# A stream of weight jobs spread over the attention tiles, with another last tile for its planner

## The chip, the cores and the metric

The kernel runs on one core of a Trainium2 chip. The metric is the device time of one execution in microseconds (us), lower is better. One execution was recorded by the hardware profiler; its times are counted from the first instruction of the span.

## The reference

Attention with rotary embedding (4 batches, 8 heads, 576 positions, head size 64), then a layer that takes the maximum of three products, then a layer with SiLU. All weights are dense; no routing takes place.

```python
q_rot, k_rot = rotate(q), rotate(k)
scores = scale * np.matmul(q_rot, k_rot.transpose(0, 1, 3, 2))
attn = np.exp(scores - max(scores)) ; attn = attn / (sum(attn) + 1e-09)
x = matmul(attn, v)                       # as 2304 tokens x 512
h = np.maximum(np.maximum(x @ w1, x @ w2), x @ w3)     # 512 -> 768
y = h @ w_out                                          # 768 -> 512
g = y @ w_in ; g = g * (1.0 / (1.0 + np.exp(-g)))      # 512 -> 2048
out = g @ w_out2                                       # 2048 -> 512
```

## The kernel before

Products that need accuracy are done as three passes of 16-bit floats: each operand is split into a high and a low part, and high x high, high x low and low x high are summed. Weights arrive as 64-bit floats, and are narrowed on the chip.

**The attention** is a list of 80 tiles, 20 for each batch: for a pair of heads and 128 queries a tile has scores on TensorE (`tile_scores`, L443, L433 and L434, in one PSUM tile s with a single buffer), the maximum on VectorE (`tile_max`, L453), exponentials on ScalarE (L460), the norm (`tile_norm`, L470 and L472), moves of the probabilities by SP's DMA queue (`tile_move`, L511), a transpose within blocks on VectorE (`tile_flip`, L533) and the product with the values (`av`, tile xp, L578). `attention()` is a generator; at step j it issues the scores and the maximum of tile j and the later parts of the tiles before it. It has five steps more than tiles, for the parts that trail. From tile 25 on (`LOOSE`) the scores of a tile are queued behind the last matmul group that was issued before.

**The first layer** of earlier batches runs between the tiles: the main loop draws groups of matmuls (L673) from `moe_groups()`, from tile 25 on in portions of three passes, as far as a debt of TensorE columns (`pace`) allows. Rotations of later queries and keys (`rope_steps`, L366 to L370) run on GpSimd. The groups of the last batch run behind the loop, for the most part in PSUM tiles mg, which take the place of the attention's; the second layer (`moe2`) comes last.

**The weight jobs** are the stream that the change touches. `side_jobs()` yields them one by one, with their planned cost in ns of VectorE time:

- `narrow_w2(WI, ...)`: 32 units that bring the weight w_in of the second layer to 32 bits. A unit is a load (L874), a cast on ScalarE (L229), three operations on VectorE (L241, planned 420; L248 and L249, planned 820), a sum of squares on ScalarE (L155) and a store to DRAM (L845, or L850 for the second weight). At the end the scale of the weight is found: a row maximum wm on VectorE (L263), a transpose (L122), a maximum (L124) and a broadcast (L130) on TensorE, four small operations on VectorE, planned 600.
- `narrow_w2(WO, ...)`: the same for w_out, whose loads and stores are in GpSimd's queue, and between its units the 16 items of `prep_w8`: a load of za, sums on GpSimd (L989), two high parts on ScalarE (L966), two low parts on VectorE (L970, planned 730 each) and two stores of w8o (L997) to w8scr, where the second layer will read them.

**The planner** gives every step an allowance. `busy(j)` estimates VectorE's other work in step j, and `SIDE` is one constant for all steps: the whole planned cost of the jobs and of the other work, divided by the number of steps. In each step from `LOOSE` on the debt `side_debt` grows by `SIDE - fixed[j - 1]`, and jobs are issued as long as it is positive. What is left after the loop is issued at once:

```python
            if j > LOOSE:
                side_debt += SIDE - fixed[j - 1]
...
            drawn = j > LOOSE and side_debt > 0 and side_next is not None
            if drawn:
                side_debt -= max(side_next, 0)
...
    for _ in side:
        pass
```

The order in which an engine takes its instructions is settled before the run, by a scheduler that places what was issued along a timeline of its own; an engine then works through its queue in that order.

Of the kernel before, what the change touches and what calls it, by code (L numbers as in the profile page):

```python
# [22 lines left out]
def fused_kernel(  # L23
# [568 lines left out]
    tiles, events, first, x_ready, av_at = [], {}, {}, {}, {}  # L592
# [10 lines left out]
    for i, (b, hp) in enumerate(pairs):  # L603
        u = first[b, hp]
        if b > 1:
            j = first[b, 0] + 3 * hp - 7
# [18 lines left out]
    LOOSE = 25  # L625
    LAST = [(B - 1, hp, t) for hp in range(NP) for t in PARTS[1][2]]

    def attention():

        back = lambda j, n: tiles[j - n] if n <= j < len(tiles) + n else None  # L630
        for j in range(len(tiles) + 5):
            b_now[0] = int(j > LOOSE)
            if j < len(tiles):
                with tc.issue_after(last["group"]) if j > LOOSE else nullcontext():
                    tile_scores(tiles[j])
                tile_max(tiles[j])
            for n in (3, 2):
                key = back(j, n)
                if key and moved(key[0]) and n == 3 - (key in LAST):
                    tile_flip(key)  # L640
            for a in av_at.pop(j, ()):
                av(*a)
            key = back(j, 1)
            if key:
                tile_norm(key)
                if moved(key[0]):
                    tile_move(key)
            key = back(j, 2)
            if key:
                (tile_last if moved(key[0]) else tile_turn)(key)  # L650
            for f, a in events.pop(j, ()):
                f(*a)
            yield
# [696 lines left out]
    def side_jobs():  # L1350


        yield from narrow_w2(WI, wi2, "wi")
        items, n, done = prep_w8(1.7), 0, 0
        for cost in narrow_w2(WO, wo2, "wo"):
            yield cost
            n += cost < 0
            while done < n / 1.25:
                x = next(items, None)
                if x is None:  # L1360
                    break
                if x < 0:
                    done += 1
                else:
                    yield x
        yield from items

    def busy(j):


        half = lambda i: 0 <= i < len(tiles) and tiles[i][2] == 4
        full = lambda i: 0 <= i < len(tiles) and tiles[i][2] != 4
        ns = 1350 * full(j) + 750 * half(j) + 150 * (j <= len(tiles)) + 230 * half(j - 2) + 500 * len(av_at.get(j, ()))
        for n in (2, 3):
            if j - n < len(tiles) and n == 3 - (tiles[j - n] in LAST):
                ns += 700 if half(j - n) else 1240
        ns += sum({qk_turn: 700, v_max: 800, v_scale: 150, v_scale_b: 600}.get(x[0], 0) for x in events.get(j, ()))
        return ns + max(pace[j], 0) * 530 // 3840

    side, side_debt, side_next = side_jobs(), 0, -1  # L1380
    fixed = {j: busy(j) for j in range(LOOSE, len(tiles) + 5)}
    SIDE = (60 * 1240 + 32 * 730 + sum(fixed.values())) // len(fixed)
    for j, _ in enumerate(attention(), 1):
        step[0] = j
        if moe is None:
# [10 lines left out]
        if x_p.get(1) is not None:  # L1396
# [4 lines left out]
            if j > LOOSE:  # L1401
                side_debt += SIDE - fixed[j - 1]
        debt = min(debt + (pace[j - 1] if j > LOOSE else RATE), 3 * RATE)
# [104 lines left out]
```

## Time and profile before

| | |
|---|---|
| median of 3 runs | 981.9 us (979.5 to 985.38) |
| profiled execution | 979.38 us, span 977.7 us |
| TensorE busy | 899.6 us, 92% |
| VectorE busy | 714.6 us, 73% |
| ScalarE busy | 609.2 us, 62% |
| GpSimd busy | 469.1 us, 48% |
| mean granted TensorE clock | 0.980 |

A share of busy time is an average over stages. Engines are named PE (TensorE matmuls), PEld (TensorE weight loads), DVE (VectorE), ACT (ScalarE), POOL (GpSimd) and SP (SyncE, which issues DMAs). A tile's name without its number stands for all its buffers. Matmuls overlap, so that the duration of one is longer than the distance to the next.

### The profile page before, as it was taken

How to read it: one execution, taken by the hardware profiler on the slowest of the kernel's cores; microseconds unless marked ns; L12 is line 12 of the kernel's file. 1: busy time of each engine (PE TensorE's matmuls, PEld its weight loads, DVE VectorE, ACT ScalarE, POOL GpSimd, SP SyncE). 2: the span in 40 equal slices, each digit the busy share in tenths (PEclk: the TensorE clock that was granted, in tenths of full speed). 3: DMA queues.
4: the chain of work that ended last, by engine and by line, in shares of the span. 5: the costliest groups of instructions: out<-in, count | busy, mean ns of one | idle time of the engine just before them, and what ended most of it. 6: DMA issues, size and time to landing. Idle time of an engine off the chain costs nothing.

```text
span 977.7 us, 19067 instructions
## 1 busy us (share of the span) xinstructions
PE 899.6 (92%) x6802; PEld 667.8 (68%) x6802; DVE 714.6 (73%) x1271; ACT 609.2 (62%) x1405; POOL 469.1 (48%) x546
## 2 busy tenths in 40 slices
PE   3877998989999999999998498999998999999997
PEld 1443664656667566666655386788887888888886
DVE  6779887887788778877777856365786867856554
ACT  1988577757778678788777544363554545545342
POOL 6744584960335414322233635164486467464363
PEclk9798999999999999999999799999999999999999
DMA  6943034958878998889878862173543434424101
GB/s 152 286 142 107 17 109 125 192 120 174 189 174 185 223 173 193 215 162 190 204 194 210 294 214 88 42 227 126 163 156 99 134 121 135 122 90 135 61 1 44
DMA packets 173679, 146.30 MB, mean 150 GB/s; under 512 B 50960, under 2 KB 156176, under 8 KB 173584
## 3 DMA queue, kind: packets, MB, share of 16 engines
q1 hardware_dynamic: 167984, 131.77, 53.5%
q0 software_dynamic: 4096, 12.59, 4.5%
q8 instruction: 54, 0.88, 0.4%
q10 hardware_dynamic: 1504, 0.72, 0.3%
q14 instruction: 41, 0.34, 0.1%
HBM read 90.51 MB, written 26.21 MB: 119 GB/s over the span
## 4 chain that ended last, share of the span: by engine, by line
PE 50%; DMA 8%; DVE 8%; ACT 5%; SPq 3%; issue 3%; POOL 2%; DVEq 0%; ACTq 0%; POOLq 0%
PE m L1121 8%; PE m L673 8%; PE mb L1121 6%; PE c L1184 4%; PE a L1184 4%; PE b L1184 4%; DMA pt<-e 3%; PE mg L673 3%; PE s L443 2%; PE xp L578 2%; SPq L511 2%; PE d L1184 2%; ACT e L460 2%; DVE nb L453 2%; POOL gsum L1068 1%
## 5 line engine op out<-in xcount | busy, mean ns | idle before, releaser
L673 PEld LDWEIGHTS <-w 128*128 128x128 f16 x1632 | 159.6, 99 | 61.6 <-issue 17.5
L673 PE MATMUL m<-x,w 128*128 128x256 f16 (+1 forms) x1348 | 185.4, 287 | 8.8 <-DVE t L704 4.3
L1184 PEld LDWEIGHTS <-g 128*128 128x128 f16 x1485 | 146.0, 98 | 17.6
L1121 PEld LDWEIGHTS <-w8s 128*128 128x128 f16 x1344 | 131.1, 98 | 16.1 <-issue 0.9
L460 ACT ACTIVATE e<-s,nb 128x576 f32<-128x576 f32 x144 | 105.2, 735 | 38.6 <-DVE nb L453 35.1
L453 DVE TENSOR_REDUCE nb<-s 128x2 f32<-128x1152 f32 (+1 forms) x80 | 98.5, 1232 | 37.9 <-PE s L443 33.4
L472 ACT ACTIVATE e<-e,rec 128x576 f32<-128x576 f32 x144 | 104.0, 766 | 13.4 <-DVE rec L470 11.8
L366 POOL TENSOR_TENSOR w<-qk,sin_sb 128x512 f32<-128x512 f32 (+2 forms) x40 | 41.9, 1049 | 81.2 <-DMA qk<-in_q_dram 57.9
L443 PE MATMUL s<-T 64*128 64x512 f32 x256 | 77.6, 685 | 0.0
L578 PE MATMUL xp<-pt,vd 128*64 128x256 f32 (+1 forms) x512 | 76.1, 414 | 0.9 <-DVE pt L533 0.7
L533 DVE STREAM_TRANSPOSE pt<-pt 128x1024 f32<-128x1024 f32 (+1 forms) x60 | 67.5, 1127 | 7.4 <-DMA pt<-e 7.4
L1135 POOL TENSOR_TENSOR z<-t 128x256 f32<-128x256 f32 x32 | 27.2, 850 | 89.8 <-DVE t L1127 54.1
L874 POOL DMA_DIRECT2D z<-in_moe_w_out_dram x32 | 17.8, 555 | 107.0 <-ACT junk L155 24.4
L1073 DVE SCALAR_TENSOR_TENSOR g<-gsum,sg,g 128x1024 f16<-128x1024 f32 x36 | 49.1, 1371 | 22.5 <-ACT g L1072 22.1
L673 PE MATMUL m<-h,wo 128*128 128x256 f16 (+1 forms) x448 | 63.7, 290 | 0.4 <-POOL wo L175 0.3
L1072 ACT ACTIVATE g<-gsum,sg 128x1024 f16<-128x1024 f32 x36 | 40.8, 1141 | 37.1 <-POOL gsum L1068 37.1
L673 PEld LDWEIGHTS <-wo 128*128 128x128 f16 x512 | 50.1, 99 | 17.2 <-issue 2.7
L578 PEld LDWEIGHTS xp<-pt,vd 128*64 128x64 f32 x512 | 35.2, 136 | 32.8 <-issue 9.8
L1184 PE MATMUL c<-w,g 128*128 128x256 f16 x376 | 48.6, 276 | 0.0
L1184 PE MATMUL b<-w,g 128*128 128x256 f16 x376 | 48.5, 273 | 0.0
L1184 PE MATMUL a<-w,g 128*128 128x256 f16 x376 | 48.4, 274 | 0.0
L367 POOL TENSOR_TENSOR qk<-qk,cos_sb 128x512 f32<-128x512 f32 (+2 forms) x44 | 46.8, 1067 | 2.7
(268 smaller groups left out, 2009.6 us busy)
## 6 DMA issues: line engine op xcount, KB each, us to landing
w8s<-w8scr SPq DMA_DIRECT2D x64, 448.0 KB, 4.2
pt<-e SPq DMA_DIRECT2D x192, 128.0 KB, 4.1
z<-in_moe_w_in_dram SPq DMA_DIRECT2D x32, 256.0 KB, 3.7
z<-in_moe_w_out_dram POOLq DMA_DIRECT2D x32, 256.0 KB, 4.3
w8scr<-w8o SPq DMA_DIRECT2D x32, 256.0 KB, 3.8
w<-in_moe_w_dram SPq DMA_DIRECT2D x6, 768.0 KB, 5.4
wo<-in_moe_w_dram SPq DMA_DIRECT2D x6, 768.0 KB, 4.5
qk<-in_q_dram SPq DMA_DIRECT2D x32, 128.0 KB, 3.6
```

The lines of the kernel that those rows point to most:

```text
L366: tt(out=w4, in0=t4, in1=sin2, op=ALU.mult)
L367: tt(out=t4, in0=t4, in1=cos2, op=ALU.mult)
L443: last["s"] = last["score"] = nc.tensor.matmul(s[:, o:o + 512], qs[r], kt[r], start=True, stop=True).ins
L453: x = nc.vector.tensor_reduce(out=nb[:, 0:m], in_=both(s, 0, 960, 576) if m > 1 else s[:, 0:576], op=ALU.max, axis=AX.X, negate=True)
L460: x = nc.scalar.activation(out=e[:, HK[g]], in_=s[:, SK[g]], func=AF.Exp, bias=nb[:, g:g + 1], accum_out=sm[:, g:g + 1])
L472: nc.scalar.activation(out=e[:, HK[g]], in_=e[:, HK[g]], func=AF.Copy, scale=r[:, g:g + 1])
L533: nc.vector.transpose(out=x, in_=x)
L578: nc.tensor.matmul(xp[r, 0:n], v4[:, g, c, :], turned(c, g), start=False, stop=(c == 3))
L673: x = nc.tensor.matmul(ps[:, 0:n], l, r, start=(first and i == 0), stop=(not more and i == len(passes) - 1))
L1073: nc.vector.scalar_tensor_tensor(out=l, in0=x, scalar=sg_t[jb], in1=h, op0=ALU.mult, op1=ALU.subtract)
L1121: nc.tensor.matmul(o, l, r, start=(i == 0), stop=(i == len(passes) - 1))
L1184: x = nc.tensor.matmul(ps, l, r, start=first, stop=last_, skip_group_check=True)
```

## The change

The estimate of the other work is taken over the 80 tiles alone, and the five steps behind them count as free of other work (0). The whole cost now counts 61 units instead of 60 and both scales, and is divided by the 55 tiles from `LOOSE` on, instead of by the 60 steps from `LOOSE` on. The jobs, their order among themselves and the loop that draws them stay as they are.

```diff
     side, side_debt, side_next = side_jobs(), 0, -1
-    fixed = {j: busy(j) for j in range(LOOSE, len(tiles) + 5)}
-    SIDE = (60 * 1240 + 32 * 730 + sum(fixed.values())) // len(fixed)
+    fixed = [busy(j) for j in range(len(tiles))] + 5 * [0]
+    SIDE = (61 * 1240 + 32 * 730 + 2 * 600 + sum(fixed[LOOSE:])) // (len(tiles) - LOOSE)
     for j, _ in enumerate(attention(), 1):
```

## Rows read from the trace of the kernel before

**Rows 1.** Stretches: from:to and length, busy us, TensorE clock, DMA share, GB/s.

```profile
205.00:524.00 319.00, 313.49 (x2110) 201.25 (x2110) 253.41 (x484) 247.94 (x697) 99.24 (x144) 1.00 0.86 183
258.00:330.00 72.00, 71.35 (x496) 47.70 (x497) 61.41 (x110) 53.40 (x158) 40.33 (x43) 1.00 0.85 187
524.00:563.00 39.00, 23.96 (x162) 15.97 (x159) 31.94 (x72) 21.85 (x58) 24.10 (x41) 0.81 0.92 287
563.00:631.00 68.00, 65.39 (x516) 50.78 (x514) 37.69 (x66) 27.59 (x46) 20.72 (x29) 0.98 0.33 105
```

**Rows 2.** Waits from 524 to 563: us in total, times, longest.

```profile
PE tr L122 <- DVE wm L263: 7.8, 1, 7.8
...
ACT w8o L966 <- DMA w8scr<-w8o: 4.3, 5, 2.1
...
PE m L122 <- DVE ym L165: 2.6, 1, 2.6
PE m L673 <- ACT t L727: 2.4, 1, 2.4
```

**Rows 3.** Timeline of TensorE, 531 to 569: start, us.

```profile
532.04 3.73 PE L673 MATMUL m<-h,wo 128*128 128x320 f16 x16
...
536.10 2.34 PE L673 MATMUL m<-h,wo 128*128 128x320 f16 x16
...
562.67 0.58 PE L673 MATMUL mg<-x,w1f 128*128 128x256 f16 x2 [0.25 <-DVE swoe L145]
...
563.70 4.48 PE L673 MATMUL mg<-x,w 128*128 128x256 f16 x31
...
568.56 7.48 PE L673 MATMUL mg<-x,w 128*128 128x256 f16 x67
```

**Rows 4.** Groups by line, 524 to 563: busy us, mean ns, idle before.

```profile
L249 DVE SCALAR_TENSOR_TENSOR z<-z,z 128x256 int32<-128x256 int32 x10 | 5.5, 570 | 0.0
...
L970 DVE SCALAR_TENSOR_TENSOR w8o<-za,wihalf,w8o 128x512 f16<-128x512 f32 x6 | 5.2, 861 | 0.7 <-ACT w8o L966 0.7
...
L970 DVE SCALAR_TENSOR_TENSOR w8o<-zs,wihalf,w8o 128x512 f16<-128x512 f32 x5 | 4.5, 903 | 0.1
```

**Rows 5.** Groups of VectorE by line, 435 to 524.

```profile
L249 DVE SCALAR_TENSOR_TENSOR z<-z,z 128x256 int32<-128x256 int32 x13 | 5.7, 442 | 0.1
L241 DVE TENSOR_SCALAR z<-z 128x256 uint16<-128x256 uint16 x12 | 5.2, 432 | 0.0
...
L970 DVE SCALAR_TENSOR_TENSOR w8o<-za,wihalf,w8o 128x512 f16<-128x512 f32 x6 | 4.3, 722 | 0.0
L248 DVE TENSOR_SCALAR z<-z 128x256 int32<-128x256 int32 x13 | 3.9, 303 | 0.0
```

**Rows 6.** Waits from 200 to 524: us in total, times, longest.

```profile
DVE nb L453 <- PE s L443: 26.6, 20, 3.6
...
DVE nb L453 <- PE s L434: 4.2, 6, 1.4
...
DVE pt L533 <- DMA pt<-e: 3.8, 2, 2.8
```

**Rows 7.** Timelines: end of a tile's exponentials and the next scores, first and last pair.

```profile
208.18 0.20 ACT L460 ACTIVATION_READ_ACCUMULATOR e<-s,nb 128x1 f32 x1
...
211.13 0.38 PE L440 MATMUL s<-kd,T 128*128 128x128 f32 x2
...
521.55 0.20 ACT L460 ACTIVATION_READ_ACCUMULATOR e<-s,nb 128x1 f32 x1
...
521.80 1.12 PE L433 MATMUL s<-T,qd 128*128 128x512 f32 x2 [1.17 <-ACT e L460]
```

**Rows 8.** Groups of VectorE by line, 258 to 330.

```profile
L249 DVE SCALAR_TENSOR_TENSOR z<-z,z 128x256 int32<-128x256 int32 x12 | 8.8, 737 | 0.1
L241 DVE TENSOR_SCALAR z<-z 128x256 uint16<-128x256 uint16 x11 | 8.5, 775 | 0.1
```

**Rows 9.** Timeline of VectorE: the last tile's maximum.

```profile
523.57 0.75 DVE L453 TENSOR_REDUCE nb<-s 128x1 f32<-128x576 f32 x1
```

## The prediction

> **What bounds the kernel now.** I read the busy times by stretch first, because the change moves work from one stretch into another. From 205 to 524 us the 55 tiles run on which the planner spreads the weight jobs; there TensorE is busy for 313.5 of 319 us at full clock, VectorE for 253.4, ScalarE for 247.9, GpSimd for 99.2. So matmuls bound that stretch, and VectorE has 65.6 us spare. From 524, when the last tile has its scores, to 563 it is another kernel: TensorE works for 24.0 of 39 us at a mean granted clock of 0.81, while VectorE is busy for 31.9. From 563 on TensorE is nearly full again [rows 1].
>
> Next the waits of the weak stretch. The longest by far is one transpose (L122, tile tr) that stands 7.8 us behind the row maximum wm of the second weight, the last result of the weight jobs. Another stands 2.6 us behind ym, which VectorE reaches only after the weight work queued ahead of it, and a down group stands 2.4 us behind its eviction on ScalarE, which has itself waited 4.3 us for staging tiles w8o to be stored [rows 2]. Behind that transpose stand the mg groups of the last batch, which begin only at 562.67 [rows 3]. So the weight jobs set the end of this stretch, and attention and the groups do not.
>
> **What the change does, step by step.** It changes two constants of a planner and no instruction. I followed the loop with its own arithmetic. busy(j) sums to 220,467 ns over tiles 25 to 79 and to 8,663 over the five steps after them. Before: SIDE = (60 x 1240 + 32 x 730 + 229,130) / 60 = 5448. After: (61 x 1240 + 32 x 730 + 1200 + 220,467) / 55 = 5830. A step's allowance for weight jobs, SIDE less its own busy, rises on average from 1439 to 1821 ns of planned VectorE time, by 27%. Walking the generator with both: the first weight's 32 units end in step 45 instead of 50, the second begins in 46 instead of 51, and the stream ends in step 80 with the scale of wo. Before, steps 81 to 85 and the loop behind them still held 9 units, 12 low parts of w8 and that scale: 9 x 1240 + 12 x 730 + 600 = 20.5 us as planned, against 55 x 382 ns = 21.0 us of added allowance. The groups' portions are drawn from another debt, and their order on TensorE does not move.
>
> *What leaves the drain.* By the trace it held 10 units (L241, L248 and L249 once each) and 11 low parts (L970, six from za and five from zs) [rows 4]. With them gone, TensorE's idle time there, 39.0 - 24.0 = 15.0 us, has no cause left but the attention's own tail. The clock comes on top: 16 matmuls of 320 columns took 3.73 us behind an idle gap and 2.34 us a little later, 1.4 us lost; the 31 mg matmuls behind the long gap took 4.48 us, while 67 later ones took 7.48, 0.112 each, so 31 are worth 3.5 and with the five ahead of them about 1.2 us are lost [rows 3]. At most 15.0 + 2.6 = 17.6 us can come back. I keep 2.5 us of it for what stays: the ym step (2.6 us idle before it [rows 2]), for which other groups could stand in, and the wait for the last move of the probabilities, now with little behind which to hide. Bounds of this term: 0 kept, or half of the idle time, 7.5 us. **Gain 15.1 us.**
>
> *What enters the attention.* In VectorE time a unit costs 0.44 + 0.43 + 0.30 = 1.18 us in the late tiles and a low part 0.72 [rows 5] (0.86 and 0.90 in the crowded drain [rows 4]). 10 x 1.18 + 11 x 0.72 = 20 us, 0.36 us a tile, and as much again on ScalarE (a cast and a square for each unit, a cast for each low part; that engine has 71 us spare [rows 1]). Is there cover? VectorE stood idle for scores 26 times in the 54 tiles from 200 us on, 30.8 us in all [rows 6]: in these tiles the added work fills a wait. In the other half the maximum starts later by some 0.4 us. That reaches TensorE only where the next scores follow at once on the exponentials, since the score tile has one buffer. I measured that gap for the 53 tiles from the one whose exponentials end at 208.38 (next scores 211.13) to the last but one, 521.75 (next scores 521.80) [rows 7]: it averages 1.3 us, and 14 of 53 are under 0.1. Pushing all 53 later by 0.3 us would add 4.3 us of TensorE stall, by 0.5 us 7.4, by 0.8 us 13; at 0.4 in half of them it is about 3 us. TensorE's whole idle time there is now 319.0 - 313.5 = 5.5 us [rows 1], so this adds half of it again. The scale of wo moves into step 80, where TensorE has attention work queued behind its transposes; I add 1.5 us. **Loss 4.5 us**, bounds 0 (all hidden in waits for scores) and 20 (all of the moved VectorE time on the path).
>
> *Queues.* On SP's queue about 18 issues (stores of w8o, loads of za) now stand among the moves of pt, on GpSimd's some 10 loads of z and as many stores beside the last ropes. VectorE waited for landed probabilities only twice in the tiles, 3.8 us [rows 6], and the share of the DMA engines there is 0.86 against 0.92 in the drain [rows 1]. I cost them at nothing; the cover is the step or two between a move and its flip, and if it goes, each late flip holds VectorE by some 2 us.
>
> *A shared port.* In the stretch 258 to 330, where GpSimd turns the queries and keys of batch 2, L249 took 737 ns and L241 775 [rows 8], against 442 and 432 in the late tiles [rows 5]. So a unit there costs 1.8 us, and by the loop's walk that stretch gets about three units more: 5.5 us against 10.6 us that VectorE has free [rows 1]. The Trainium skill (SBUF — State Buffer, section "SBUF: two separate sides") says that VectorE and GpSimd share a port pair as an exclusive lock, held for a whole instruction. The longer rows agree with it. By that rule the crowding speaks against moving units into tiles that hold ropes; what it would do is the third rival.
>
> **Sum.** 979.4 - 15.1 + 4.5 = 968.8 us for the profiled execution. The three runs shown have a median of 981.9, 2.5 above it, and spread over 5.9; I add half of that: **970 us**. About 0.5%, 5 us, is what a measurement of this kernel can tell from no change.
>
> **Rivals.**
> *VectorE becomes the bound of the tiles* (the other side). All 20 us land on the path, with 2 more for the lock and 1.5 for the scale: 979.4 - 15.1 + 23.5 = 988. It decides from two thirds of the moved time on: then the gain is gone. For it: the tiles in which the maximum already waits for VectorE's queue. Against it: TensorE loses 5.5 us of 319, and VectorE waits 30.8 us for scores. Chance 0.07.
> *The drain stays latency-bound.* The last tile's chain (exponentials, norm, move, flip, AV) or the y load that needs its memory holds TensorE, and half of the idle time stays: 979.4 - 10.1 + 4.5 = 974, up to 978 if the clock falls again too. For it: flips wait on moves in the tail already. Against: the portions of batch 2 and the first groups of batch 3 are there to fill it. Chance 0.14.
> *The lock takes more.* The three units among the ropes, and those beside the ropes of batch 3, go on the path at full price, 5 us more: 974. Chance 0.12.
> *The stream trails anyway.* It is held by its own rings (three w8o tiles, four z tiles), not by the planner, and the drain keeps most of its length: 978 to 983. For it: ScalarE's 4.3 us for w8o stores. Against: that wait is not seen in the tiles, where jobs are further apart. Chance 0.07.
> The forecast has the remaining 0.60, with its own range 962 (the loss at nothing, little kept) to 976.
>
> **How the numbers follow.** Faster by over 0.5% (under 977): the forecast, the lock and most of the latency case, 0.79. Within: the trailing stream and the rest, 0.14. Slower: 0.07. The range 959 to 980 leaves out the first and the last rival and a little below.
>
> **What would show it.** In the changed profile the last L453 should start near 528 instead of 523.57 [rows 9]; the first mg matmul near 550 or before instead of 562.7; no tr L122 wait of several us; no L241 and at most a few L970 behind the last L453; TensorE's clock near 1.0 through the drain; DVE busy in the tiles at 85% instead of 79%. From 563 on everything should only be shifted. A last L453 at 540 or later makes the first rival true; a first mg beyond 558 with few weight jobs behind the last scores makes the second.

## The result and the profile after

The kernel after takes 975.05 us, the median of six runs (972.46 to 977.36), against 983.0 for six runs of the kernel before (979.5 to 985.38): a ratio of 0.9917 [0.9891, 0.9943]. It is faster, by 0.8% where 1.2% had been forecast, and lies inside the range. The profiled execution took 973.82 us, 5.6 less than that of before; the medians are 8.0 apart.

The stretches, cut at the maximum of the 27th tile, at that of the last tile and at the first mg matmul (columns as in [rows 1]), then two stretches for later use:

```profile
204.83:540.06 335.23, 318.25 (x2125) 202.46 (x2126) 274.75 (x525) 260.81 (x736) 120.05 (x180) 1.00 0.86 195
540.06:558.52 18.46, 16.90 (x127) 11.31 (x126) 8.61 (x22) 6.89 (x18) 0.31 (x1) 1.00 0.68 140
...
258.00:335.00 77.00, 70.49 (x483) 46.04 (x481) 68.34 (x128) 56.24 (x169) 42.74 (x48) 1.00 0.93 200
563.00:631.00 68.00, 67.40 (x544) 52.99 (x542) 43.54 (x75) 29.37 (x50) 36.86 (x36) 1.00 0.41 133
```

The drain is mended. It lasted 39.1 us, from 523.57 [rows 9] to 562.67 [rows 3]; now it lasts 18.5, and TensorE is idle in it for 18.46 - 16.90 = 1.6 us instead of 15.0, at full clock. The timeline of TensorE shows the scale of wo, with one short wait, and the mg groups behind it:

```profile
543.19 2.34 PE L673 MATMUL m<-h,wo 128*128 128x320 f16 x16
...
546.18 0.27 PE L122 MATMUL tr<-ident,wm 128*1 128x128 f32 x1
...
550.96 0.38 PE L130 MATMUL tr<-amax,ones 1*128 1x1 f32 x2 [1.56 <-DVE amax L124]
...
558.52 0.39 PE L673 MATMUL mg<-x,w1f 128*128 128x256 f16 x2
...
559.08 3.55 PE L673 MATMUL mg<-x,w 128*128 128x256 f16 x31
```

The wait of 7.8 us in front of L122 [rows 2] is gone, the same 31 mg matmuls take 3.55 us instead of 4.48, and 16 matmuls of 320 columns 2.34 from the start, where the first 16 took 3.73 [rows 3].

The tiles pay for it. In them TensorE is now idle for 335.23 - 318.25 = 17.0 us, where [rows 1] had 5.5. The last maximum starts 16.5 us later than in [rows 9]:

```profile
540.06 0.76 DVE L453 TENSOR_REDUCE nb<-s 128x1 f32<-128x576 f32 x1
```

The first mg matmul comes only 4.2 us earlier: 20.6 us less drain, 16.5 us more attention. Of the 17.1 us by which the tiles grew (335.2 against 318.1 between the same two maxima) 11.5 are idle time of TensorE; in the rest it works, on matmuls of the first layer among others that ran in the drain before. By tiles, 26 to 45 lose 5.2 us (1.2 before), 45 to 65 lose 5.6 (2.1) and those from 65 on 6.2 (2.2); most of the growth lies from tile 35 to 55, 8.9 us against 1.5.

The waits from 205 to 540 (as in [rows 6]) name what is new:

```profile
DVE nb L453 <- PE s L443: 20.4, 11, 3.4
...
DVE pt L533 <- DMA pt<-e: 12.7, 5, 4.3
...
PE s L433 <- ACT e L460: 6.2, 6, 1.7
...
PE s L440 <- ACT e L460: 4.7, 4, 2.0
```

VectorE waits for scores 11 times instead of 20, so that more of the tiles are set by VectorE. The scores wait for exponentials for 10.9 us in all (2.2 + 1.7 before). And the flips L533 wait 12.7 us for landed probabilities, where they waited 3.8 [rows 6]; 11.0 of it lie behind 475. There VectorE's own queue stands still, on the engine that got some 20 us of work more. The moves themselves are hardly slower: from issue to landing the moves (L511) of the tiles from 65 on take 3.9 us before and 4.0 after, as a median.

Two places show where the time goes. From 258 to 335 VectorE is busy for 68.34 of 77 us, and its integer operations are slow, as in [rows 8]:

```profile
L249 DVE SCALAR_TENSOR_TENSOR z<-z,z 128x256 int32<-128x256 int32 x16 | 10.7, 671 | 0.1
L241 DVE TENSOR_SCALAR z<-z 128x256 uint16<-128x256 uint16 x15 | 10.6, 707 | 0.9 <-ACT z L229 0.9
L248 DVE TENSOR_SCALAR z<-z 128x256 int32<-128x256 int32 x16 | 7.6, 476 | 0.0
```

One late maximum in this stretch shows how that reaches TensorE. VectorE's timeline, then GpSimd's and TensorE's:

```profile
293.08 1.51 DVE L241 TENSOR_SCALAR z<-z 128x256 uint16<-128x256 uint16 x1
...
294.74 1.35 DVE L249 SCALAR_TENSOR_TENSOR z<-z,z 128x256 int32<-128x256 int32 x1
...
298.95 0.42 DVE L711 TENSOR_TENSOR h<-t,h 128x256 f16<-128x256 f32 x1 [1.49 <-ACT h L710]
299.30 1.35 DVE L453 TENSOR_REDUCE nb<-s 128x2 f32<-128x1152 f32 x1
```

```profile
293.00 1.27 POOL L367 TENSOR_TENSOR qk<-qk,cos_sb 128x512 f32<-128x512 f32 x1
294.35 1.46 POOL L370 TENSOR_TENSOR qk<-qk,w 128x512 f32<-128x512 f32 x1
```

```profile
302.29 0.49 PE L440 MATMUL s<-kd,T 128*128 128x128 f32 x2 [2.05 <-ACT e L460]
```

L241 and L249 begin within 0.4 us of the start of a GpSimd operation and end some 0.3 us after its end; then comes a wait for ScalarE. The maximum starts 2.4 us after its scores are there, the exponentials follow it, and the next scores, which need the score tile, find TensorE idle for 2.05 us. At 330.12 another maximum starts 2.6 us late, behind an L249 of 1.95 us and the row maximum of the first weight, whose first operation waits 1.83 us for a sum of squares on ScalarE.

Late in the attention VectorE stands still while it has work queued. Its timeline from 512 to 526:

```profile
512.07 0.48 DVE L704 SCALAR_TENSOR_TENSOR t<-m,t 128x320 f32<-128x320 f32 x1
516.82 1.25 DVE L533 STREAM_TRANSPOSE pt<-pt 128x1024 f32<-128x1024 f32 x1 [4.27 <-DMA pt<-e]
...
518.69 0.16 DVE L470 RECIPROCAL rec<-rec 128x2 f32<-128x2 f32 x1
...
519.15 1.35 DVE L453 TENSOR_REDUCE nb<-s 128x2 f32<-128x1152 f32 x1
...
525.61 1.25 DVE L533 STREAM_TRANSPOSE pt<-pt 128x1024 f32<-128x1024 f32 x1 [1.36 <-DMA pt<-e]
```

and those of ScalarE and of SP's queue beside it:

```profile
518.88 1.44 ACT L472 ACTIVATE e<-e,rec 128x576 f32<-128x576 f32 x2
```

```profile
508.22 6.03 SPq L511 DMA_DIRECT2D pt<-e  x8
520.35 2.65 SPq L511 DMA_DIRECT2D pt<-e  x4
```

Read it as a ring. The flip waits from 512.5 to 516.8 for its probabilities to land. The reciprocal of a following tile and the next maximum are queued behind it and run only at 518.7 and 519.2; the norm on ScalarE follows at 518.9, the move of that tile is issued from 520.4 to 523.0, and the next full flip waits for it again at 525.6. A late move makes a late flip, which makes the next norm and so the next move late. For the last 12 tiles (`LAST`) `attention()` issues the flip two steps behind the scores, ahead of the next tile's norm; for those before it is three, behind that norm, and a move has a step more to land.

### The profile page after: what moved, and what is told of

Same layout as the page of the kernel before. It is cut to its first block, busy times and chain, and to the rows that moved or that the text cites. A ratio compares the mean times of both kernels' runs of the same rounds, so it can differ in the third digit from the quotient of the medians.

```text
span 972.1 us, 19053 instructions
## 1 busy us (share of the span) xinstructions
PE 900.0 (93%) x6802; PEld 666.4 (69%) x6802; DVE 718.3 (74%) x1271; ACT 606.1 (62%) x1405; POOL 477.8 (49%) x546
## 4 chain that ended last, share of the span: by engine, by line
PE 53%; DMA 11%; DVE 7%; ACT 6%; SPq 4%; issue 4%; POOL 2%; DVEq 0%; ACTq 0%; POOLq 0%
PE m L673 9%; PE m L1121 8%; PE mb L1121 6%; DMA pt<-e 5%; PE c L1184 4%; PE a L1184 4%; PE b L1184 4%; PE mg L673 4%; PE xp L578 2%; PE s L443 2%; SPq L511 2%; PE d L1184 2%; ACT e L460 2%; DMA w8scr<-w8o 1%; ACT e L472 1%
## 5 line engine op out<-in xcount | busy, mean ns | idle before, releaser
L453 DVE TENSOR_REDUCE nb<-s 128x2 f32<-128x1152 f32 (+1 forms) x80 | 98.6, 1232 | 30.0 <-PE s L443 28.3
L533 DVE STREAM_TRANSPOSE pt<-pt 128x1024 f32<-128x1024 f32 (+1 forms) x60 | 67.6, 1129 | 18.0 <-DMA pt<-e 17.6
L443 PE MATMUL s<-T 64*128 64x512 f32 x256 | 80.8, 693 | 0.0
L962 POOL TENSOR_TENSOR z<-z 128x256 f32<-128x256 f32 x32 | 31.8, 1019 | 39.6 <-DMA z<-zwo 33.7
```

The lines of the kernel that those rows point to most:

```text
L443: last["s"] = last["score"] = nc.tensor.matmul(s[:, o:o + 512], qs[r], kt[r], start=True, stop=True).ins
L453: x = nc.vector.tensor_reduce(out=nb[:, 0:m], in_=both(s, 0, 960, 576) if m > 1 else s[:, 0:576], op=ALU.max, axis=AX.X, negate=True)
L533: nc.vector.transpose(out=x, in_=x)
```

## The experiments

Three explanations of the loss stood against each other: **VectorE's time**, dear among the ropes; **the ring** of waits in the late tiles; **SP's queue**, in which the stores of w8o stand among the moves. All runs in one table (medians; each ratio is to runs of before on the same chip; idle is TensorE's, from the maximum of the 27th tile to that of the last, and from there to the first mg matmul):

| kernel | median us | ratio to before | last L453 | first mg | idle in tiles | idle in drain |
|---|---|---|---|---|---|---|
| before | 983.0 | | 523.57 | 562.67 | 5.5 | 15.0 |
| after | 975.05 | 0.9917 [0.9891, 0.9943] | 540.06 | 558.52 | 17.0 | 1.6 |
| e1_half | 970.21 | 0.9866 [0.9824, 0.9907] | 537.60 | 558.07 | 5.4 | 5.1 |
| e2_no_low | 973.11 | 0.9897 [0.9862, 0.9933] | 537.41 | 557.34 | 14.0 | 1.6 |
| e3_no_rope2 | 970.18 | 0.9854 [0.9818, 0.9890] | 536.46 | 554.85 | 13.9 | 1.5 |
| e4_late | 974.83 | 0.9897 [0.9852, 0.9942] | 536.20 | 554.07 | 13.3 | 0.3 |
| e5_store_pool | 975.54 | 0.9913 [0.9888, 0.9939] | 541.73 | 560.01 | 16.7 | 1.4 |
| e6_last_lag | 967.53 | 0.9843 [0.9798, 0.9887] | 538.65 | 555.14 | 3.4 | 2.6 |
| e7_no_ropes | 964.81 | 0.9825 [0.9772, 0.9879] | 529.01 | 547.42 | 11.2 | 1.5 |
| e8_low_lag | 960.01 | 0.9772 [0.9724, 0.9821] | 531.01 | 545.71 | 2.0 | 1.7 |
| e9_late_lag | 966.93 | 0.9841 [0.9793, 0.9890] | 540.61 | 551.46 | 7.6 | 0.0 |
| e10_before_lag | 981.49 | 0.9994 [0.9969, 1.0018] | 522.83 | 564.16 | 2.4 | 20.5 |
| e11_half_lag | 967.7 | 0.9852 [0.9829, 0.9874] | 533.31 | 553.87 | 2.6 | 5.5 |
| e12_act_low | 970.43 | 0.9875 [0.9842, 0.9909] | 537.90 | 555.62 | 8.8 | 2.4 |

The first 205 us differ by some 4 us between profiled executions with the same work there (the 27th maximum starts between 204.7 and 209.3; at 203.0 in e3 and 200.4 in e7, which lack ropes there). So idle times between two events of one execution are compared, and starts only roughly.

**e2_no_low**: the low part's first operation is left out of every unit, the most that a cheaper unit could win.

```diff
-                with tc.issue_after(last["max"]):
-                    W.narrow_low(part.get(n - 3))
```

> The changed kernel without the operation L241 of every weight unit (the low bits of the narrowed weights are left out; loads, stores, casts and the planner's steps stay). Three theories of why the tiles ended 16.5 us later in the changed kernel (last L453 at 540.1 instead of 523.6, TensorE idle 16 us instead of 5.5 in the tiles). A, VectorE time: some 30 units in the tiles lose 0.4 to 0.8 us each there, 55 units in all about 28 us of 284, so VectorE is lighter than in the kernel before; last L453 near 525, about 960 to 963 us. B, the lock among the ropes of batch 2: the 15 units there lose 0.7 us each, 10 us, so TensorE's 6.5 us of idle time between 258 and 335 goes to about 2; about 966 to 968. C, moves that land late because of more DMAs: nothing of that changes, last L453 near 538, 972 to 975.

Measured: 973.11, 2 us under the kernel after and not told apart from it. The idle time of tiles 35 to 45 falls from 5.2 to 0.9 us, but tiles 65 to the last keep 8.5 (6.2 with the change). Less work on VectorE shrinks the early loss and not the late one; the flips wait no less, 14.9 us.

**e3_no_rope2** and **e7_no_ropes**: GpSimd's ropes of batch 2, then those of batches 2 and 3, are left out.

```diff
+        if b == 2:
+            return None
...
+        if b > 1:
+            return None
```

> The changed kernel without the rotation of batch 2's queries and keys (nine GpSimd operations for each of four pairs are left out), so that no GpSimd work of that kind meets the units between 258 and 335. A: only the crowding there goes, a third of TensorE's idle time in the tiles; about 969 to 971. B: L249 falls from 671 ns to about 440 there and L241 from 707 to 430, TensorE's idle time from 258 to 335 from 6.5 us to 1 or 2, the whole kernel 5 us faster, 968 to 970, and the idle time behind 365 stays. C: no change in the idle time of the late tiles, and little between 258 and 335; 973 to 975.

> The changed kernel without the rotations of batches 2 and 3 (36 GpSimd operations for each batch are left out): in the run without those of batch 2 the stretch 258 to 335 still held three pairs' rotations, which belong to batch 3. Lock (B): L241 and L249 fall to 440 to 480 ns between 258 and 335, TensorE's idle time from tile 35 to 55 goes from 9.0 us to 1 or 2, as in the kernel before (1.5); 966 to 969. A without a lock: they stay above 600 ns, the idle time stays at 4 or more; 970 to 972. D: the last 14 tiles keep 6 us of idle time in either case.

e3 left L249 at 670 and L241 at 631 ns between 258 and 335: the ropes that run there are for the most part those of batch 3, which the scheduler placed early, and not those of batch 2, as the prediction had it. (In the changed kernel three of batch 2's four pairs are turned by 211 and the fourth by 267; the three from 285 to 334 stand in e3 as well.) In e7 they are gone, and the same operations (by line, 258 to 335) are back at their price of the late tiles [rows 5]:

```profile
L249 DVE SCALAR_TENSOR_TENSOR z<-z,z 128x256 int32<-128x256 int32 x16 | 7.0, 435 | 0.1
L241 DVE TENSOR_SCALAR z<-z 128x256 uint16<-128x256 uint16 x15 | 6.5, 434 | 0.7 <-ACT z L229 0.7
L248 DVE TENSOR_SCALAR z<-z 128x256 int32<-128x256 int32 x16 | 5.0, 312 | 0.0
```

GpSimd's work beside them costs these 47 operations 28.9 - 18.5 = 10.4 us. The idle time from tile 35 to 55 falls only from 8.9 to 4.8 us. The time is 10 us under that of after, but some 4 to 5 of that lie ahead of tile 26, where ropes are missing too. Most of the late idle time stays (6.4 us from tile 55 on, against 8.0), and so do the flips' waits there (10.8 us from 470 to the last maximum).

**e5_store_pool**: the stores of w8o go through GpSimd's queue instead of SP's.

```diff
-                nc.sync.dma_start(out=w8scr[:, f, c, :, a:a + 4], in_=w[a])
+                nc.gpsimd.dma_start(out=w8scr[:, f, c, :, a:a + 4], in_=w[a])
```

> The changed kernel with the stores of w8o issued from GpSimd's queue instead of SP's, which carries the moves of the probabilities. A and B: nothing much changes, 973 to 977. C, in its form that SP's queue is late: moves go out earlier, VectorE's waits for pt (12.7 us in the tiles, 3.8 before the change) fall to about 5, 968 to 971.

Measured: 975.54, and the flips wait 11.9 us (12.7 in the kernel after). The stores in SP's queue are not the cause. VectorE, ScalarE and TensorE take their instructions in the same order as in the kernel after, up to the last maximum, and this second execution repeats the losses: 4.9, 3.0, 2.5 and 6.2 us in the tiles from 35, 45, 55 and 65 on, against 5.2, 3.8, 1.8 and 6.2.

**e4_late**: the old allowance up to step 50, and all that is added behind it, where no rope of this crowd is in the way.

```diff
-    SIDE = (61 * 1240 + 32 * 730 + 2 * 600 + sum(fixed[LOOSE:])) // (len(tiles) - LOOSE)
+    SIDE = [5448] * 50 + [(32 * 1240 + 32 * 730 + 2 * 600 + sum(fixed[50:])) // 30] * 35
...
-                side_debt += SIDE - fixed[j - 1]
+                side_debt += SIDE[j - 1] - fixed[j - 1]
```

> The first weight at the old allowance (5448 up to step 50), the second faster so that it also ends in step 80: no added units among the ropes of batch 2, all of the 20 us in steps 51 to 80. A: the late tiles take all of the added VectorE time, some 0.7 us a tile instead of 0.38, and the loss stays as large or grows; 974 to 979. B: the loss of the first half goes and the second half pays what it has room for; 969 to 972. C: the DMAs are denser in the late tiles, where flips follow their moves by one step less; worst case, 976 to 981.

Measured: 974.83, no change. Up to tile 45 TensorE loses 0.1 us, from 55 on 12.2 (after: 8.0). The work left one crowd and made the other worse.

**e6_last_lag**: the flips of the last 12 tiles come three steps behind, as everywhere else, behind the norm of the next tile. The work is the same, but the edit does a second thing: with the last products a step later, less of the other work counts among the 80 tiles (219,527 ns instead of 220,467), so that SIDE falls from 5830 to 5813, and from tile 33 on VectorE and ScalarE take their instructions in another order.

```diff
-        lag = int(moved(b) and (b, r) != (B - 1, 1))
+        lag = int(moved(b))
...
-    LAST = [(B - 1, hp, t) for hp in range(NP) for t in PARTS[1][2]]
+    LAST = []
```

> The changed kernel with the probabilities of the last twelve tiles turned (L533) three steps behind their scores, as all others are, instead of two, and the last products a step later. A theory D now stands beside A: the late part of the loss is a ring of waits in these twelve tiles, in which VectorE waits in a flip for a move to land, the reciprocal of the next tile stands behind it, so the norm and the next move are late too. D: TensorE's idle time in the last 14 tiles goes from 6.1 us to 2 or 3, VectorE's waits for pt from 12.7 to 4, ScalarE's for the reciprocal from 7.3 (443 to 540) to 2; last L453 near 536, the drain perhaps 2 us longer; 970 to 973. A alone: no change in the tiles, a longer drain; 975 to 978.

Measured: 967.53, 7.5 us under the kernel after. The stretch of the tiles, the stretch of the ropes and the wait of the flips:

```profile
209.28:538.65 329.37, 326.01 (x2174) 208.78 (x2175) 272.40 (x525) 262.20 (x742) 117.74 (x178) 1.00 0.88 201
...
258.00:335.00 77.00, 75.82 (x514) 49.14 (x511) 71.72 (x129) 59.93 (x178) 43.79 (x48) 1.00 0.84 197
```

```profile
DVE pt L533 <- DMA pt<-e: 2.9, 3, 1.7
```

TensorE is idle for 3.4 us of these 329.4, and for 0.6 from tile 55 on. From the 27th maximum to the last the stretch is 5.9 us shorter than in the kernel after, and 7.8 us more of matmuls lie in it (326.0 against 318.25). The flips' three waits lie before 350, and there is none in the last tiles. In VectorE's timeline a maximum and then a flip follow each other without a wait:

```profile
514.61 1.36 DVE L453 TENSOR_REDUCE nb<-s 128x2 f32<-128x1152 f32 x1
515.88 1.24 DVE L533 STREAM_TRANSPOSE pt<-pt 128x1024 f32<-128x1024 f32 x1
```

So the late waits hang on the flip's place. But the idle time from tile 35 to 55 fell as well, from 8.9 to 2.7 us, and there the flip did not change; only the order did. In the stretch of the ropes VectorE is busier than in the kernel after (71.72 us against 68.34), the 45 weight operations in it cost 30.3 us, and TensorE is idle for 1.2 us instead of 6.5. The 7.5 us are therefore not the ring's alone.

**e8_low_lag** (e2 and e6 together) asks whether the two edits together take away the whole loss, **e10_before_lag** whether the late flip wins something of its own, in the kernel before.

> Both at once: L241 left out of every unit and the late flip. If VectorE's time in the first two thirds and the ring of the last tiles are the whole loss, TensorE's idle time in the tiles comes down to 4 us or less (5.5 before the change, 16 to 17 after it), the last L453 to 526 to 530, and the time to 962 to 967. If something else holds the tiles, 969 or more.

> The kernel before, with the late flip of the last twelve tiles alone. If the ring of waits was made by the added jobs (D as a loss of the change), there is little to win: its last 14 tiles had 2.2 us of idle time, and the weight jobs end the drain as they did; 979 to 983. If the ring cost as much before the change and was only hidden in the drain, no gain either, since the drain's end is set by the weight jobs. A gain of 5 us or more would say that the late flip is worth its price by itself, and that the ring is no part of the change's loss.

e8 (its tiles):

```profile
206.50:531.01 324.51, 322.54 (x2174) 208.16 (x2175) 253.61 (x468) 262.07 (x742) 117.03 (x179) 1.00 0.88 204
```

2.0 us idle, with VectorE at the 253.6 us that it had before the change [rows 1], and 960.01 us: with part of the weight work left out, nothing of the loss is left. Since e6 alone comes to 3.4 us, this does not show two causes that add up; alone the edits won 2 and 7.5 us, together 15. e10 is at 0.9994 [0.9969, 1.0018]: without the added work the early flip costs nothing.

**e1_half**: half of the added allowance. **e11_half_lag** adds the late flip to it.

```diff
-    SIDE = (61 * 1240 + 32 * 730 + 2 * 600 + sum(fixed[LOOSE:])) // (len(tiles) - LOOSE)
+    SIDE = 5640
```

> The changed kernel with SIDE at 5640, half way between 5448 and 5830, so that about half of the moved jobs stay behind the last scores. If the loss in the tiles grows with the VectorE time put there, TensorE's idle time in the tiles is 9 to 12 us (5.5 and 16), the drain 26 to 32 us long (39 and 18.5), and the time 975 to 981. If the late ring of waits is set off by the last steps alone, the tiles lose as much as in the changed kernel and the time is above 979.

> SIDE at 5640 and the late flip. If the ring is the larger part of what the full allowance costs, the full allowance with the late flip (967.5) stays ahead: 970 to 975 here. If VectorE's time is, half the allowance is as good or better: 963 to 968.

I had the gain and the loss both halved, and missed: e1 is faster than that, and e11 came out at the upper end of its second case. e1's tiles and its drain:

```profile
208.80:537.60 328.80, 323.40 (x2161) 206.98 (x2162) 263.28 (x503) 257.30 (x722) 112.73 (x166) 1.00 0.88 191
537.60:558.07 20.47, 15.40 (x104) 9.89 (x104) 18.20 (x41) 12.51 (x33) 7.89 (x14) 0.92 0.86 255
```

Half of the added work, some 10 us of VectorE time in the tiles, costs TensorE nothing there (5.4 us idle, as before the change), while the drain's idle time falls by two thirds, to 5.1 us. All of it, in the changed kernel, costs 11.5 us. With the late flip the half dose gives 967.7, no better than the full dose with it (967.53). e1 and e11 have one allowance and one order up to tile 71. From there the flips' waits, 5.3 us in e1, are gone in e11, but TensorE's idle time in the last 14 tiles falls only from 1.5 to 0.5 us: with half the work most of these waits are hidden.

**e9_late_lag** (e4 and e6 together) and **e12_act_low** (e6, and the low part of every second unit on ScalarE, its planned cost cut to match) look for a version that wins more.

```diff
+                if n % 2:
+                    yield 420
+                    with tc.issue_after(last["max"]):
+                        W.narrow_low(part.get(n - 3))
...
-                    W.narrow_a(n - 2, part.get(n - 2), low=False)
+                    W.narrow_a(n - 2, part.get(n - 2), low=n % 2 == 1)
...
-    SIDE = (61 * 1240 + 32 * 730 + 2 * 600 + sum(fixed[LOOSE:])) // (len(tiles) - LOOSE)
+    SIDE = (61 * 1030 + 32 * 730 + 2 * 600 + sum(fixed[LOOSE:])) // (len(tiles) - LOOSE)
```

> The old allowance for the first weight, the rest in steps 51 to 80, and the late flip, with all of the computation: a version that could be kept. If D explains the late part, its last 14 tiles go from 7.7 us of idle time (in the run with the old first half alone) to 4; 968 to 972. If the denser late tiles are held by VectorE's time itself, no gain over that run's 974.8.

> The changed kernel with the late flip, and with the low bits of every second weight unit made on ScalarE instead of VectorE (SIDE computed with 1030 ns a unit, so that the stream still ends in step 80). All of the computation is kept. If VectorE's time is what is left of the loss once the ring is gone (967.5 with the late flip alone, 960.0 with L241 left out altogether), half of that comes back: 962 to 966. If ScalarE, at 77% in the tiles, has no room for 0.4 us more in every second unit, nothing is gained or some is lost: 967 to 972.

e9 takes 966.93 us, 7.9 less than e4. The order of VectorE is e4's up to tile 55; behind it the flips' late waits are gone, and the idle time of the last 14 tiles falls from 7.7 to 0.2 us. The drain is 10.9 us long without idle time, but tiles 45 to 65 lose 7.3, so that e9 ends level with e6. e12 is no better than e6, 970.43: ScalarE is busy for 277 of the 331 us of its tiles, and scores wait for the exponentials (waits of its tiles):

```profile
PE s L433 <- ACT e L460: 5.5, 6, 2.5
```

The best versions that keep the whole computation are e9, e6 and e11, at 966.93 to 967.7, not told apart from one another. Each beats both kernels, and before by 1.5%.

## Why the prediction came out right, with its loss too small

**The bound** was read rightly. Taking the weight jobs out of the drain took away its idle time, and no flip, y load or fallen clock held TensorE in their place.

**The gain** came out as summed: 15.0 - 1.6 = 13.4 us of idle time, where 12.5 were forecast (2.5 kept), and the clock's 2.6 nearly as the rows had it (1.4 us in the 16 matmuls of 320 columns, 0.9 in the 31 of mg). About 16.0 against 15.1.

**The loss is the term that was mis-sized.** Of the 4.5 us forecast, 1.5 were the wait at the scale of wo; it came, with 1.6 us, but in the drain, where it is counted above. For the tiles 3.0 us were forecast and 11.5 measured. 979.4 - 16.0 + 11.5 = 974.9; the execution took 973.8. The sum for this execution had been 968.8; the time still lies inside 959 to 980 because that range had room for a loss of this size. Two parts of the term were wrong.

First, "the maximum starts later by some 0.4 us" in half of the tiles is a mean, and the loss does not follow the mean. From tile 35 to 55 it grew from 1.5 to 8.9 us, with the three longest waits, 1.4 to 2.1 us, each behind one late maximum. Beside GpSimd a unit is some 0.67 us dearer in L249, L241 and L248 (671 - 435, 707 - 434, 476 - 312). The prediction saw that price and gave it a rival with 5 us of its own; the likeliest sum left it at nothing. It also gave it to the wrong ropes. e7 shows that GpSimd's work makes the difference in price: the same 47 operations take 28.9 us beside it and 18.5 without it. The Trainium skill (SBUF — State Buffer, section "SBUF: two separate sides") has an exclusive lock on the port pair, held for a whole instruction, for a VectorE operation with two inputs in SBUF or in a two-port mode. The L249 of 1.35 us, which ends 0.3 us after a GpSimd operation of 1.46, agrees with it; no trace tells in which mode L241, with one input, ran.

Price and amount alone do not make the loss, though. Taking away some of either shrinks it: half the work (e1, 2.2 us from tile 35 to 55), none of it added up to step 50 (e4, 1.1), a cheaper unit (e2, 3.2), no ropes (e7, 4.8). But e6, with all of the work, dearer operations and VectorE busy for 93% of the stretch from 258 to 335, loses 2.7. So it matters too what stands ahead of which maximum, and a mean over the tiles cannot say that.

Second, "*Queues* ... I cost them at nothing". The price behind it was named rightly, some 2 us for each late flip (12.7 us for five waits), but not when the cover goes. The cover was a step or two between a move and its flip; in the last 12 tiles it is a step less, and there the flip stands in VectorE's queue ahead of the reciprocal that the next move depends on. Once one move is late, so are those after it. That can be read off the order in `attention()` without a run. The late flip was put into five kernels, and each time the late flips' waits up to the last maximum went; TensorE's idle time in the last 14 tiles fell from 6.2 to 0.0 us (after to e6), 8.5 to 0.0 (e2 to e8), 7.7 to 0.2 (e4 to e9), 1.5 to 0.5 (e1 to e11) and 2.2 to 0.1 (before to e10). So the ring is shown for these tiles, and so is that it takes the added work to make it dear; e5 shows that the stores in SP's queue have no part in it. Of the 11.5 us it accounts for about 4 (6.2 against 2.2), the tiles from 35 to 55 for 7.4.

**The signs that were named.** The last maximum came at 540, not near 528, which was the sign of the first rival, VectorE as the bound. Half of that rival came true: more tiles wait for VectorE. But it is busy for 82% of them (274.75 of 335.23; 85% was forecast), and late in them what holds the tiles is its waits for landings, not its work. TensorE's first mg at 558.5 was the sign of the second rival, but the drain is full of matmuls: the mark was reached because the tiles ended late. Signs should have been intervals, and not points of time. Behind 563 all is only shifted: L1089 starts at 625.7 (631.5 before).

**Open.** Which feature of the order costs the tiles from 35 to 55 their time in the changed kernel and not in e6: the two differ in 17 ns of allowance a step, in the flips of the last tiles and in what the scheduler made of that, and no run changed the order alone. For the same reason e6's 7.5 us are not divided between the ring and the order. Why the scheduler runs the ropes of batch 3 so early, and whether placing them elsewhere wins some of e7's 10 us, was not tried.

## What to carry to other kernels

Work moved out of a drain into a busy stretch does not cost by its mean. Here half of it cost nothing (e1 and e11), and the whole cost 11.5 us of idle time in one order of the queues and nothing in another, with the late flip (e6): try half the dose, and another placement of the whole, before calling an engine full. Before filling an in-order queue, look in it for an instruction that waits for a DMA ahead of one on which the next such DMA depends; with slack it is harmless, without it a ring closes, and one step more of distance opens it. When an experiment touches a planner, compare the order of the instructions too: an edit to the last 12 tiles reordered the queues from tile 33 on.

## What the runs showed of the hardware

Integer operations on VectorE ran longer beside GpSimd's tensor operations, with one tile operand as with two. From 258 to 335 in the changed kernel the L249 that overlapped none took 0.40 to 0.43 us, and those that overlapped one up to 1.95. The means with e7's and the changed kernel's rows side by side: 434 to 707 ns (L241, one operand), 435 to 671 (L249, two), 312 to 476 (L248, one). L248 is not always hit: in the kernel before, from 258 to 330, with the L249 and L241 beside it at 737 and 775 [rows 8], it kept its price.

```profile
L248 DVE TENSOR_SCALAR z<-z 128x256 int32<-128x256 int32 x12 | 3.8, 313 | 0.0
```

TensorE kept its full clock through a drain of 18.5 us in which it was idle for 1.6; in e6's of 16.5 us, idle for 2.6, the mean was 0.90, and with 15.0 of 39 idle it was 0.81 [rows 1].
